# Gated linear attention and a PReLU MLP on one core: the first unit's phases and decays placed by TensorE products

## The chip, the cores and the metric

The kernel runs on one core of one Trainium2 chip. The metric is the device time of one execution in microseconds (us). A second kind of number is the span in a profile, from the first to the last instruction of one profiled execution.

## The reference, cut to what matters

```python
# q, k, v, a_re, a_im: (4 batches, 8 heads, 768 tokens, 48 channels), float32
mag = np.sqrt(a_re * a_re + a_im * a_im)
scale = np.minimum(mag, 0.999) / (mag + 1e-06)
a_re_n, a_im_n = a_re * scale, a_im * scale          # a complex gate per token and channel
for t in range(S):                                    # S_re, S_im: (B, H, 48, 48), start at zero
    new_re = ar * S_re - ai * S_im                    # ar, ai: the gate of token t, per key channel
    new_im = ar * S_im + ai * S_re
    S_re, S_im = new_re + k[t] (outer) v[t], new_im
    y[t] = q[t] @ S_re
x = y as (3072 tokens, 384)                           # heads side by side
h = x @ w_in                                          # w_in (384, 2048)
g = np.maximum(h, 0) + alpha * np.minimum(h, 0)
out = g @ w_out                                       # w_out (2048, 384); both weights arrive as 64-bit floats
```

## The kernel before, in words

The 3072 tokens are cut into 24 units of 128 tokens, six per batch. A complex gate is a magnitude and an angle. The kernel sums the angles along the tokens into a phase, turns every query and key by its phase, and so is left with real decays (magnitudes), which it multiplies up in a binary tree.

- **Gates.** `gates(g, b, c0, c1)` computes phases and decays for a group of units: group 0 is the first unit alone, group 1 the next two, group 2 the other three of batch 0, and then two groups of three for each later batch. All its operations work on the tile `room`, with the 384 rows (8 heads x 48 channels) laid out as 3 blocks of 128 partitions. VectorE (DVE) and ScalarE (ACT) take turns in it: `Abs_reciprocal_sqrt` and squares (L291 to L295), the angle (L297 to L307), its running sum (L316), cosine and sine of the phase (L319 to L351, the results being the tiles `turn` and `sine`), the magnitude (L358 to L366) and the tree of decays `dec` (L376).
- **Over DRAM.** A unit wants these numbers in another layout: heads side by side in the free dimension, channels on partitions, each channel on two neighbouring partitions (96 of them). So `gates` sends `sine` and `turn` to the DRAM tile `phs` (L342) and `dec` to `decs` (L379). The task `loads` reads them back as `PP` (L538, phases: 96 partitions, 8 heads x 129) and `T` (L545, decays: two transfers, one for the even and one for the odd partitions, 8 heads x 256).
- **Units.** `unit(u)` first multiplies the loaded queries and keys `KQ` by the phases (L625, L627 on DVE), then walks six levels of the decay tree. At each level DVE multiplies `KQ` by decays (L683), ACT copies halves of it (L706, L722), and TensorE (PE) makes small products `ps_lv` (L642), which are masked (L656 on ACT, L666 on DVE). Then come a transpose of the keys (L754, with copies L756 and L757), the state (L766, L774, L777), and the outputs `ps_y` (L792, L806), copied to `T` by ACT (L814). The first two units are moved to the layout of the MLP by PE (L823, copied at L828); the others go over DRAM (`ysc`). For the first two units three levels of the values `VL` are picked out of `V` by PE products (L587, copied at L591).
- **MLP.** Pairs of units make one block of 256 tokens. The first two blocks go through `features` (PE L874, ACT L881, DVE L883) and `outputs` (L924); the other ten through `two_features` (PE L896, ACT L905 and L909, DVE L911) and a seven-product scheme (L1014 and its folds). The weights arrive as 64-bit floats in `shared` (L440) and are turned into 32-bit ones piece by piece: ACT L460, L462, L464, then DVE L468, L470. There are 8 pieces of each weight matrix.
- **What sets the order.** Every engine executes its instructions in program order. The tasks above are generators, and each letter of the string `ORDER` advances one of them by one step: A to I are the groups of gates, J `loads`, K `half_rows`, L `loads_v`, M `pieces` (the weight loads and the loads of `start` and `alpha`), N and O the conversions of the weights, P onwards the units, n `loads_x`, o the MLP. The string was made by a planner that gave each step a cost; the kernel holds only its result. The instructions ahead of the tasks (identity, masks, small constants, almost all of it on GpSimd, POOL) stand in the order in which they are written, as the scheduler of the framework leaves them. All DMAs are issued by SyncE (SP), one queue in program order: an issue that waits holds all those behind it.
- **Two small loads that the prediction names.** `start` (L408 cleared by POOL, L415 loaded by SP) and `al` (L420, L422) stand early in SP's queue, ahead of the first weights (L440).

Of the kernel before, what the change touches and what calls it, by code (L numbers as in the profile page):

```python
# [9 lines left out]
F32 = mybir.dt.float32  # L10
# [5 lines left out]
ALU = mybir.AluOpType  # L16
# [3 lines left out]
P = 128  # L20
# [10 lines left out]
    "ABKMMAABBAAAAAAMBMJAABAMMMAAAAAAAABANABABBBBAAAAAAAAAAAAAAAAJJJMAABABNNNBBBBBBBBBBJOONOOOBPPPPJJJJBP"  # L31
    "BBBBBBBBBBPPPBNONPCJBBPPBPNJMBPPPNBBLLNLPCCCPPLLLQJPQCLCNCPPPPNPOPPPPPPPLJOCOCPPPCOPQCCNCCPJLLMLCPCL"
    "LLLQMLLCCOCJCCPOOQPQQMMCQJJPPPPPPPMLQQCCCPLOOLJQQQQQLJCCCCCQoLLLQoooNNoNNNooQQQQCRoMLoRoooQLCQRCNQQQ"
    "oQQJJCDooRoooooQRRQQQROQRoOooooNoDLLLOooRNNNCRCNCoLJQCQLooLRQQRooLCLDJNDKOCoooRoooKKQQROoQoQSDDDRRRQ"
    "QooCooooNNLDQQRRRRRoooNoRoooLRooNDMLRRLLRooooooRoLJoLRSOooooODJooooooRNDOOSoooooooJKRSOoDoRSDOOSKLoS"
    "oooSSLJRMLLDSooLNooRoooOOoNRLSLLDMJJRRRRRRRMSSSSDRRRDSSLLLLLLLJTooooDoooNooLSSSSLSJSSSSoDoooooSLSoTN"
    "OoSooooLSLLLLMNSSJDSTDSNNNNNOSOOoTOoooooooSSSSSSTTooJooTSSSSOLOJTTTooooooOTnoooDooooOOODDDDTJTooooJo"
    "oLLLDDLLLDTooooooooDTUTTJDDooooooooTTTDDJLTooooTTTTTTToooooJLUoLELLLTooTLLTDTUTTTToooJoJooooEUDDoooD"
    "DDDDTUTUTTEETEEUUUETTUooVLoUooToooooUUUUoUUooooooooUUUUUUUTooEUUoooLUoULLLoLJUooUUUEEEoUVELLJLLVLLLV"
    "VLoooKEEooooUVUUUUKVVUUUKKJVJUUJJLLLLLEVLJVVooooooooJLooVoooVVVEVoEooooooLKVKKVLLLEEoKoooooooooVVVoL"  # L40
    "LLVVVLVVooVWoVnVoJJVWWooVVVVWWWWWVVVVEWEJWWoooooVVWVWVVVVVoEoWWWoWEJoooooJJoooooooooooooWLLLLLLLEEXW"
    "WWLEXLEWEJLoXJLLLLLJooEEEWooooooooWWWWoWooooXJooooooWoXXWoooWEoXooWoEWXXoooooooEEEEooooooooEEEEXWWWW"
    "XooooooWWWXXXWWWWWoXXYLLLoXooooooooooooooooXXXXXYnXoooooooooooXXXXJJXooYooooooooXXoooXXXYXYYYXoooooY"
    "oooooooooooooooFFFFFFFLXYYXLLLLLLJLLLLooooJLJooYoooooooooFXFYXYJXXXXXXYYFZFYYZoooooooooooooooooooooJ"
    "JFLLJYYYYYYLFFoooFYYYoLLLLLLLLLZoooooooooYoYoooFYoooYYYYZFZZYYZLJLFFFFFYYZZZoooooooooooFFFFZoooLJJFo"
    "KooooooooooFYYYYYYoLYYJoJZZnZLZZLLLLFFooZoooooooooooooFFFaoZZZFFFJoFoLooFZoooaaLGZZZZooooZZLKKZFFLLL"
    "LoooooaJoooooooZoZLooooooooKZZZZLFaZaoZZooaoooooooooooooooGGJJGGGaGGaaoooooooooooooooooooooGoGaZaZZa"
    "aZoooooobFooooLoooaooooooZZZZaaGaaaobaaoooooooooooooGGooaaaaaobaoaLLJJoLLLLLLLoGbaaabbbbGaGLLLLbGGbb"
    "aaJbJooGoJboooooooooaababGboJaaaaaLLbbLJJLoooooJbJLoooooooooooooooGobbbbboonKLLLLLoGbbbbbbcoJobbccJo"
    "ooooooooobcccccccoobLbooooooooooooooooobbGcdoooooLLLLooooooooooooooGGGGGbGbGcbbcbbbbKLLLLLbGLbcKoooo"  # L50
    "ooooLccLoooLJooooooooooLLoLcGccLcoJGLGcLccoooJccdHJGooGooccooooooooooccooccoccccooooooooooGGdGGooooo"
    "oooccdddddHHdJJdcoooHdooooooooooooGoooocdcdcooodeccccddooLdoooooJHoooeoonddddddddJLdooHoHHoooooooooo"
    "ooooodLLdooHoooooodooooeoodeoooodeHeeedeooooodeoooHHHHooooooooooLLooLdooooeooooLLLLLdLLddeLdJJJddedd"
    "dddLeLLLooooLJJJLJLLLJLJeeeoooHHHHoooooooooeHHLLLeHoLoooooooeeeeooooooooeeeeeHHoooHofeoHHLHefffHoooo"
    "ooooooooooooeeeffffffeoooooooJoooooooHHHoefooHHooHHHHooooooooooeefeeefeeoefffeenoHoooooofLLLoooooooo"
    "ooooooooHHHooofffffffoooooooooofJffoJooooKffofoogLLLLggIooooogooLLoooLIfggoLgogIfIgoffIIfgLLJIJIgooo"
    "oooooooooooLLooooooooooooooffgffHgfJJfKKIffffgogIoLogooooooooooghIoooggoghhLJoooooooogoooohogggggggo"
    "ogoooLJLLLLLLLLLLghJgIhILhhgggghhIoooooooooooohIoohJJIIIIJggggggggIoooJJIInooJohooooooooooooIIIIIooo"
    "ohhhhhLiLLIJiioooLLJLLLLoooIoooooohoooooooooooooooihhhIohhhhiiLLohJooooooooiioihioooooooooooohhooooo"
    "hohohihhiLLLLjooIooooooooooojhhohIhIoooooooohhihhoiihLhhhoooooooooooooLiLioiiLIIIIIiiJiiiJoIoooooooo"  # L60
    "oooooiiioiooojoiiooiiiijjjIjjjjiojiioooLLJLLLLLLLLLoooooooooiiJIjijjioooioiiiojJJLJoooonLLLooooooooo"
    "ojooJLLooLLjkooooooooojjojjjjjjjooooooooooooooooooooooooooJJJoooooooooooooooookoLLLLLLJLjjooooookjoo"
# [35 lines left out]
def kernel(  # L98
# [44 lines left out]
    MT = MC * P  # L143
    NU = B * NCH
    GT = NCH // 2 * P
    TL = 2 * P
# [7 lines left out]
    work = ctx.enter_context(tc.tile_pool(name="work", bufs=2))  # L154
# [60 lines left out]
    g_sb = shared[:, 0:18 * MT].rearrange("p (r e) -> p r e", r=3)  # L215
    place_of = shared[:, 18 * MT - 3 * P:18 * MT]
# [13 lines left out]
    scr_of = {}  # L230
# [18 lines left out]
    def gates(g, b, c0, c1):  # L249
# [87 lines left out]
        scr = dram.tile([H * D, C, TL], F32, tag="decs", name="decs")  # L337
        phs = dram.tile([H * D, 2, n + 1], F32, tag="phs", name="phs")
# [174 lines left out]

    def loads():
        for u in range(NU):
# [18 lines left out]
            loaded[u] = L = dict(KQ=KQ)  # L534
            t = yield DMA(393, ("PP", u), takes=(R["PP"],))
# [662 lines left out]
```

## Time and profile before

| What | Value |
|---|---|
| Time, median of 3 runs | 743.08 us (741.89 to 750.89) |
| The profiled execution | 746.64 us |
| Its span | 744.9 us |
| PE busy | 675.1 us (91%) |
| DVE busy | 600.8 us (81%) |
| ACT busy | 501.3 us (67%) |
| POOL busy | 14.8 us (2%) |
| DMA queue of the loads and stores | 126.94 MB, 62.6% of 16 engines |
| Mean granted clock of PE | 0.988 |

Busy shares are averages over the whole span and hide that the kernel has stages with different limits, so the stretches of the span have to be looked at one by one. "Idle before" in a row is the idle time of the engine just ahead of it and what ended that.

### The profile page before, as it was taken

To read this page: it belongs to the slowest core of one execution; us is meant where nothing else is said; L and a number is where in the kernel's file an instruction comes from. 1 tells how busy PE (TensorE), PEld (TensorE's weight loads), DVE (VectorE), ACT (ScalarE), POOL (GpSimd) and SP (SyncE) were. 2 spreads that over 40 slices of the span, in tenths; PEclk is the share of its full clock that TensorE was granted. 3 is DMA by queue.
4 is the path that set the end of the run, shared out by engine and by line. 5 is a ranking of instruction groups with operands and counts; after the bars stand their busy time and mean duration, and the time that the engine had idled before them with its cause. 6 is when DMAs were issued, how large, how long until landed. Compare 5 with 4: busy or idle time off the path is not lost.

```text
span 744.9 us, 26879 instructions
## 1 busy us (share of the span) xinstructions
PE 675.1 (91%) x11776; PEld 582.3 (78%) x11776; DVE 600.8 (81%) x791; ACT 501.3 (67%) x899; POOL 14.8 (2%) x54
## 2 busy tenths in 40 slices
PE   0036998999999999989999999999999999999998
PEld 0025676677678888878888889989888988889997
DVE  6899999989999799989887998899876666741422
ACT  7999999976667777857676677768745354353230
POOL 6000000000000000000000000000000000000000
PEclk9997899999999999999999999999999999999999
DMA  8999987897777665786767555776738425311000
GB/s 274 235 260 266 280 279 208 213 256 235 194 195 235 178 152 152 206 226 146 199 189 227 151 120 150 241 201 169 193 83 226 111 78 149 88 40 60 0 22 22
DMA packets 157693, 128.67 MB, mean 173 GB/s; under 512 B 62696, under 2 KB 147944, under 8 KB 156136
## 3 DMA queue, kind: packets, MB, share of 16 engines
q1 hardware_dynamic: 157576, 126.94, 62.6%
q8 instruction: 93, 1.52, 0.8%
q14 instruction: 24, 0.20, 0.1%
HBM read 89.91 MB, written 34.43 MB: 167 GB/s over the span
## 4 chain that ended last, share of the span: by engine, by line
PE 57%; DVE 16%; DMA 9%; ACT 4%; issue 4%; SPq 3%; DVEq 0%; ACTq 0%
PE ps_h L896 21%; PE ps_o L1014 19%; DVE KQ L683 5%; PE ps_lv L642 4%; PE ps_y L806 3%; PE ps_kv L766 3%; DMA T<-decs 2%; DMA shared<-in_w_in_dram 2%; DMA PP<-phs 2%; PE ps_y L792 2%; PE ps_o L924 2%; PE ps_kt L754 2%; PE ps_h L874 1%; SPq L578 1%; PE ps_h L1014 1%
## 5 line engine op out<-in xcount | busy, mean ns | idle before, releaser
L896 PE MATMUL ps_h<-xT,w_in_sb 128*128 128x256 f32 x960 | 229.0, 384 | 0.8 <-DMA xT<-ysc 0.8
L896 PEld LDWEIGHTS ps_h<-xT,w_in_sb 128*128 128x128 f32 x960 | 176.6, 190 | 22.9 <-issue 1.4
L683 DVE TENSOR_TENSOR KQ<-KQ,T 96x1024 f32<-96x1024 f32 x120 | 146.0, 1216 | 19.8 <-PE ps_lv L642 10.4
L1014 PE MATMUL ps_o<-w_out_sb,shared 128*128 128x192 f32 x624 | 111.3, 329 | 1.2 <-DVE top L1020 0.8
L911 DVE TENSOR_TENSOR shared<-shared,ps_h 128x512 f32<-128x512 f32 x80 | 54.6, 682 | 70.5 <-ACT shared L909 70.5
L1014 PEld LDWEIGHTS ps_o<-w_out_sb,shared 128*128 128x128 f32 x624 | 102.2, 190 | 4.1 <-DVE top L1020 1.0
L905 ACT ACTIVATE shared<-ps_h 128x512 f32<-128x512 f32 x80 | 47.7, 596 | 68.5 <-PE ps_h L896 68.1
L1014 PE MATMUL ps_o<-shared 128*128 128x192 f32 x448 | 79.2, 329 | 0.0
L706 ACT COPY WQ<-KQ 96x1024 f32<-96x1024 f32 x48 | 49.9, 1040 | 38.0 <-DVE KQ L683 37.6
L909 ACT ACTIVATE shared<-shared,al 128x256 f32<-128x256 f32 x160 | 73.1, 502 | 2.3
L1014 PEld LDWEIGHTS ps_o<-shared 128*128 128x128 f32 x448 | 73.1, 190 | 1.6 <-DVE top L1041 0.5
L642 PE MATMUL ps_lv<-WQ 96*32 96x32 f32 x2304 | 34.3, 202 | 38.2 <-DVE WQ L625 32.1
L642 PEld LDWEIGHTS ps_lv<-WQ 96*32 96x32 f32 x2304 | 26.1, 115 | 50.5 <-DVE WQ L625 32.1
L874 PE MATMUL ps_h<-xT,w_in_sb 128*128 128x256 f32 (+1 forms) x240 | 54.0, 356 | 1.2 <-issue 1.1
L924 PE MATMUL ps_o<-w_out_sb,shared 128*128 128x384 f32 x128 | 53.1, 519 | 1.9 <-DVE shared L883 1.4
L874 PEld LDWEIGHTS ps_h<-xT,w_in_sb 128*128 128x128 f32 x240 | 41.9, 202 | 14.1 <-issue 3.2
L722 ACT COPY W<-KQ 96x512 f32<-96x512 f32 x48 | 30.8, 642 | 31.4 <-DVE KQ L683 30.2
L806 PE MATMUL ps_y<-A,VL 64*48 64x64 f32 x2304 | 45.0, 221 | 0.3 <-DMA VL<-vsc 0.3
L656 ACT ACTIVATE A<-ps_lv,columns 128x64 f32<-128x64 f32 x144 | 36.6, 332 | 12.0 <-PE ps_lv L642 11.9
L814 ACT COPY T<-ps_y 48x512 f32<-48x512 f32 x48 | 27.7, 578 | 24.0 <-PE ps_y L806 23.4
L806 PEld LDWEIGHTS ps_y<-A,VL 64*48 64x48 f32 x2304 | 36.9, 120 | 7.0 <-issue 4.9
L756 ACT COPY T<-ps_kt 128x384 f32<-128x384 f32 x48 | 23.0, 479 | 23.5 <-PE ps_kt L754 23.3
(118 smaller groups left out, 975.0 us busy)
## 6 DMA issues: line engine op xcount, KB each, us to landing
T<-decs SPq DMA_DIRECT2D x48, 384.0 KB
PP<-phs SPq DMA_DIRECT2D x24, 387.0 KB
KQ<-KQ SPq DMA_DIRECT2D x23, 384.0 KB
phs<-room SPq DMA_DIRECT2D x14, 577.5 KB
decs<-room SPq DMA_DIRECT2D x7, 1152.0 KB
VL<-vsc SPq DMA_DIRECT2D x44, 144.0 KB
shared<-in_w_in_dram SPq DMA_DIRECT2D x8, 768.0 KB
shared<-in_w_out_dram SPq DMA_DIRECT2D x8, 768.0 KB
```

The costliest lines, as they stand in the source:

```text
L642: nc.tensor.matmul(t[64 * i + j:64 * i + j + HC // 2, p], lhsT=keys(n, g), rhs=queries(n, g), start=True, stop=True)
L656: nc.scalar.activation(a[:, :, cols], t[:, :, at:at + name], AF.Copy, scale=s)
L683: nc.vector.tensor_tensor(out=x, in0=x if x0 is None else x0, in1=m, op=ALU.mult)
L706: nc.scalar.copy(z.rearrange("p i n t -> p i (n t)").rearrange("p i (m h) -> p m i h", h=h), bass.AP(tensor=KQ.tensor, offset=KQ.offset + ...
L806: nc.tensor.matmul(o, lhsT=Vp[h][64 * i:64 * i + 64, s, e_ * D:(e_ + 1) * D], rhs=a, start=False, stop=(s == 1 and h == LEVELS[-1]))
L874: nc.tensor.matmul(p, lhsT=w_in_sb[:, f // 2, kk, f % 2 * P:(f % 2 + 1) * P], rhs=x_of[m][:, kk, c * P:(c + n) * P], start=(kk == 0), stop ...
L896: nc.tensor.matmul(p[:, i], lhsT=w_in_sb[:, f // 2, kk, i * P:(i + 1) * P], rhs=x_of[m][:, kk], start=(kk == 0), stop=(kk == NK - 1))
L905: nc.scalar.activation(gt, p, AF.Relu, scale=-1.0)
L909: nc.scalar.activation(some_, some_, AF.Copy, scale=al_1[:, f + i:f + i + 1])
L911: nc.vector.tensor_tensor(out=gt, in0=gt, in1=p, op=ALU.add)
L924: nc.tensor.matmul(sums[0], lhsT=gt, rhs=w_out_sb[:, f], start=(f == start), stop=(f == stop))
L1014: nc.tensor.matmul(z, lhsT=a[:, i], rhs=w[:, i], start=i == 0, stop=i == F2 - 1)
```

## The change

For the first unit (group 0 of the gates) nothing goes over DRAM any more. The last steps of `gates(0, ...)` leave `turn`, `sine` and `dec` in `room`, and a new function `nearby` places them into `PP` and `T`: PE multiplies the blocks of `room` by slices of a shifted identity matrix (`spots`), which picks the 48 rows of a head and puts each on two partitions (decays), or the cosine on the even and the sine on the odd ones (phases). Two heads share one PSUM tile of the ring `h` (two buffers). ACT copies the four pairs of `PP` and two of the four pairs of `T`; DVE copies the other two. The matrices `spots` are made by POOL at the start, one memset and three `affine_select`. `ORDER` is a new string throughout, so all steps of all tasks may stand elsewhere; the tasks and their steps are otherwise the same.

```diff
+    spots = shared[:, 0:2 * (P + D2) * 2].rearrange("p (j c) -> p j c", j=2)
+    nc.gpsimd.memset(spots, 0.0)
+    for j, i in ((0, 0), (1, 0), (1, 1)):
+        nc.gpsimd.affine_select(out=spots[:, j], in_=spots[:, j], pattern=[[1, 2 * (P + D2)]], base=-D2 - i,
+                                channel_multiplier=-2, compare_op=ALU.not_equal, fill=1.0)
+    near = {}
     place_of = shared[:, 18 * MT - 3 * P:18 * MT]
     nc.gpsimd.memset(place_of, 0.0)
...
-        done["sine", g] = yield from send(1, ts)
+        if g:
+            done["sine", g] = yield from send(1, ts)
...
-        done["turn", g] = used = yield from send(0, t)
-        for u in range(b * NCH + c0, b * NCH + c1):
-            scr_of[u] = (scr, phs, u - b * NCH - c0)
-            done["PP", u] = used
+        if g:
+            done["turn", g] = used = yield from send(0, t)
+            for u in range(b * NCH + c0, b * NCH + c1):
+                scr_of[u] = (scr, phs, u - b * NCH - c0)
+                done["PP", u] = used
+        else:
+            near["turns"], near["decays"] = (turn, sine), dec
+            done["PP", 0] = t
...
+        if not g:
+            done["T", 0] = t
+            return
         t = yield DMA(N, t)
         nc.sync.dma_start(scr.rearrange("(t p) c s -> p t (c s)", p=P),
                           dec.rearrange("p (t c) s -> p t (c s)", t=NK))
...
+    def nearby(L):
+        L["PP"] = PP = work.tile([D2, H, P + 1], F32, tag="PP", name="PP", bufs=1)
+        L["T"] = T = work.tile([P, H, TL], F32, tag="T", name="T", bufs=2)
+        for name, key, dst, w in (("PP", "rotation", PP, P + 1), ("T", "decays", T, TL)):
+            for pair in range(HP):
+                e = yield PE(0.43 * 2.5, (name, 0), takes=(R["h"],) if pair else (R["h"], R[name]), n=6)
+                z = ps.tile([P, 2, MT], F32, tag="h", name="ps_near", bufs=2)[0:D2, :, 0:w]
+                for j in range(2):
+                    at = (2 * pair + j) * D
+                    some = [(t, at - t * P) for t in range(at // P, (at + D - 1) // P + 1)]
+                    if name == "T":
+                        some = [(near["decays"][:, t], spots[:, 1, D2 + 2 * o:2 * D2 + 2 * o]) for t, o in some]
+                    else:
+                        some = [(near["turns"][i][:, t], spots[:, 0, D2 + 2 * o - i:2 * D2 + 2 * o - i])
+                                for t, o in some for i in range(2)]
+                    for k, (rhs, lhsT) in enumerate(some):
+                        nc.tensor.matmul(z[:, j], lhsT=lhsT, rhs=rhs, start=k == 0, stop=k == len(some) - 1)
+                if name == "T" and pair % 2:
+                    t = yield DVE(2 * w, e)
+                    nc.vector.tensor_copy(dst[0:D2, 2 * pair:2 * pair + 2], z)
+                else:
+                    t = yield ACT(2 * w, e)
+                    nc.scalar.copy(dst[0:D2, 2 * pair:2 * pair + 2], z)
+                R["h"].put(t)
+            done[key, 0] = t
+        done["gates", 0] = t
...
             loaded[u] = L = dict(KQ=KQ)
+            if u == 0:
+                yield from nearby(L)
+                continue
             t = yield DMA(393, ("PP", u), takes=(R["PP"],))
```

The string `ORDER` is left out of the diff. Where the two programs stand side by side below, the lines of the kernel before are named.

More of the change, by code (lines that the diff above doesn't have):

```diff
@@ L36 @@
[L36 to L50, printed above, removed]
@@ new lines @@
+    "oCRQQQQQooooooQQRCNLLNQNoCQNQQRooKDRLLQoooCNJQNCRLQDMOOOLRCRQooooRCNNNQORCOooCQoDNNQooSRoCQQooDQQQQo"
+    "RRRQQRQLLoLLLLoDDDRooRoooLQJJLLDLKJOOoooMooRRRRRRRooooRSRooLRooROoooooRDoRDoSoRRNNNooooooooRNOORSoLo"
+    "ooooDDRLLDDLJOMROROSRSSSNSoMJRRRRRNoSDOSooooooooooooSSSoSDDDSSNooooLLLLooooooNoRRMLLLLOJSSSSSooSSNNo"
+    "ooSoSSSoDooSoSoSSDoLLLLLLLSoJJMoJTTSJOONNODOSSSSSSSooSSoOTSSLooNNoNToooooTJTonLLTLJLOTOoOOOLoLJoooJo"
+    "JToTooooooDToooooLoTTTDTDDLLDDJTDDooTooooooooLDUUooooUTTTTDLLLDTDDDoTooooooToTUUTooTTDooooTooJJELoET"
@@ new lines @@
+    "oTTDTUUTDTTTUDDDUUoooooooETTTVVVUEEETDUUUUETUULLLLLoTooooooooooooLLTTUUUUULLLLLooUUoVEUUUUooLLooEJJJ"
+    "UoooUUEUUKJKEEoooKUUUEEEEEEVEooooooooVooUVUKJKVULUUVUVoUJLLLJLVooooVooJVooooVVELEoVoVVVKoooooooooooL"
+    "oVVoVoVVVVVJoJVVWWVonooWVoLLLLoVVVEWWWLJLoEooooWVooooLLooEEEoEEoooVWJVVVWooEoVVVVVVWVVoooooWLLWWWooo"
+    "WEJoWEJLWXLLLLJooooooWWWWoooLLLLLLLWWWWWXXoWWoooooooooWXWoXXXEWWWXXXoooooooooooooWWWWLJJJXXWoWXWWWEo"
+    "EWWWooooEEEEEEEXXXnLYXoooooooooooooooooooooooooooJJLLoXXXXXXXXooooooooooooXYXXooooooXooXFLLLLooooLLL"
@@ new lines @@
+    "LYXXXXoooooooooooooFFYFYYYYXXXFYLLLYLJoFFooooooooYoKJXXYXYJYJXXXXXLFoooYYYooooooooooooLJoooYFFYJFYoo"
+    "YYLLLLLLLLoYLLooooooooKooooZLYFFYZYYYooYooYYYFFooLLooKKooooFYYZFZFJoJFooYKKKJJoooooooooYYZZYFZFoooFZ"
+    "ZZoFFFFFZKoooooooooooooooooFYZYZYYYYYooZoZZFooFooZLLLLnoooooFooooooaFZZoZFoFoZoooFoFFFaFZoooooZZoooo"
+    "oooJJLLLooooooZZZZGLLLLLLLLKooooZZJJooaFFZZZZooaZooooooooooooooooooZZaZaaZFGoGGGGGaaaoooooooooooooJJ"
+    "GooZaaaaZZZooLLaaaoooooooooooooooaaooaoaaoobbGaaaaaaZZLooLLooLLaaoJoooooooJLLLLaaabbbKGooooooooooaba"
@@ L336, in gates @@
             nc.scalar.copy(carry, turn[:, :, n])
-        scr = dram.tile([H * D, C, TL], F32, tag="decs", name="decs")
-        phs = dram.tile([H * D, 2, n + 1], F32, tag="phs", name="phs")
+        if g:
+            scr = dram.tile([H * D, C, TL], F32, tag="decs", name="decs")
+            phs = dram.tile([H * D, 2, n + 1], F32, tag="phs", name="phs")
         def send(o, after):
```

47 lines of the change are left out of this document (24 added, 23 removed).

## The prediction

> **What bounds the kernel now.** The page comes first, with the busy time and share of each engine.
>
> ```profile
> PE 675.1 (91%) x11776; PEld 582.3 (78%) x11776; DVE 600.8 (81%) x791; ACT 501.3 (67%) x899; POOL 14.8 (2%) x54
> ```
>
> PE leads, but not everywhere, so I cut the span into stretches. The columns are the stretch, its length, then busy us of PE, weight load, DVE, ACT and POOL, the clock granted to PE, the DMA share and GB/s.
>
> ```profile
> 0.00:20.00 20.00, 0.00 (x0) 0.00 (x0) 14.04 (x37) 15.74 (x26) 12.49 (x34) 1.00 0.91 271
> 20.00:32.10 12.10, 0.00 (x0) 0.00 (x0) 9.97 (x16) 11.92 (x16) 0.19 (x2) 1.00 1.01 229
> 32.10:40.00 7.90, 1.51 (x78) 1.24 (x82) 7.41 (x12) 7.84 (x10) 0.10 (x1) 1.00 0.95 229
> 40.00:65.00 25.00, 11.77 (x404) 9.67 (x398) 24.96 (x29) 24.33 (x36) 0.00 (x0) 0.99 0.97 283
> 65.00:82.00 17.00, 14.28 (x171) 11.56 (x172) 16.67 (x19) 16.85 (x28) 0.41 (x1) 0.51 1.08 271
> 82.00:110.00 28.00, 26.17 (x524) 20.16 (x526) 27.39 (x44) 26.72 (x49) 0.00 (x0) 1.00 0.96 268
> 110.00:150.00 40.00, 36.02 (x804) 27.43 (x796) 39.70 (x56) 37.58 (x62) 0.11 (x1) 1.00 0.82 218
> 150.00:700.00 550.00, 544.38 (x9601) 473.72 (x9600) 447.71 (x563) 352.02 (x663) 1.52 (x15) 1.00 0.60 164
> ```
>
> Two regimes: from 150 us PE idles 5.6 of 550 us, and whatever delays its work there delays the end. Before about 80 us PE is starved: it does nothing for 32.1 us, while ACT and DVE, from 20 us on, hardly pause. ACT idles 0.18 us between 20.0 and 32.1, and 0.67 + 0.15 + 1.28 = 2.1 us between 40 and 110. So the first MLP work comes when ACT and DVE have got through what stands ahead of it in their queues.
>
> Next, whether the trip over DRAM is what the first unit waits for. Its first DVE operation is L625, its first use of `T` L683:
>
> ```profile
> 29.98 0.96 DVE L470 CUSTOM_DVE_ANT_0 w_out_sb<-top,w_out_sb 128x1536 uint16<-128x1536 uint16 x1
> 30.85 1.21 DVE L625 TENSOR_TENSOR WQ<-KQ,PP 96x1024 f32<-96x1024 f32 x1
> 32.10 1.22 DVE L627 TENSOR_TENSOR KQ<-KQ,PP 96x1024 f32<-96x1024 f32 x1
> 33.24 0.55 DVE L691 TENSOR_TENSOR St<-St,start 96x384 f32<-96x384 f32 x1
> 33.71 1.21 DVE L683 TENSOR_TENSOR KQ<-WQ,T 96x1024 f32<-96x1024 f32 x1
> ...
> 34.93 0.85 ACT L364 ACTIVATE room<-room 128x768 f32<-128x768 f32 x1
> 35.68 0.64 ACT L722 COPY W<-KQ 96x512 f32<-96x512 f32 x1
> ```
>
> No row has an idle bracket. DVE comes to L625 straight from converting a weight, to L683 straight from L691; ACT comes to L722, the first copy of the unit, straight from the gates of group 1 (L364). `PP` and `T` were there in time: the trip is hidden behind the queues.
>
> **The change part by part.** *Order.* I set the two programs' instruction orders side by side and counted what each engine must do ahead of some landmarks. Ahead of the first L722, ACT has exactly the same operations in both, plus six copies out of `ps_near`. Ahead of the second unit's L625, and of the ninth feature's L883, DVE has the same plus two copies. So nothing of groups 1 and 2 and no weight is moved behind the first unit; at other landmarks up to the first `two_features` the sum differs by some 3 us either way. I take 0, bounds -3 and +3.
>
> *Removed.* Seven transfers: two `phs` writes, one `decs` write (as large as one read of `T`), `PP`, and two reads of `T`.
>
> ```profile
> T<-decs SPq DMA_DIRECT2D x2, 384.0 KB
> ...
> phs<-room SPq DMA_DIRECT2D x2, 193.5 KB
> PP<-phs SPq DMA_DIRECT2D x1, 387.0 KB
> ```
>
> Together 387 + 384 + 387 + 768 = 1926 KB, 1.97 MB, 7.3 us of the queue at 271 GB/s. The first unit did not wait for them, so directly they bring 0; they make room for what follows, at most 7.3 us. The next part gives that back.
>
> *Added on POOL, and with it on SP.* Here I expect most of the harm. SP issues the load of `start` only when POOL has cleared it, and `al` and all weights stand behind that issue.
>
> ```profile
> 0.94 0.42 POOL L217 MEMSET shared<- 128x384 f32 x1
> 1.44 0.29 POOL masks.py:199 TENSOR_SCALAR_AFFINE_SELECT ident<-ident 128x128 f32<-128x128 f32 x1
> 1.67 0.12 POOL L408 MEMSET start<- 96x32 f32 x1
> 1.73 0.20 POOL L173 MEMSET mask<- 128x128 f32 x1
> 1.88 0.49 POOL L220 COPY shared<-ident 48x48 f32<-48x48 f32 x2
> 2.44 0.58 POOL L228 COPY shared<-ident 128x64 f32<-128x64 f32 x3
> 2.98 1.13 POOL L174 TENSOR_SCALAR_AFFINE_SELECT mask<-mask 128x128 f32<-128x128 f32 x1
> ...
> 2.54 0.64 SPq L415 DMA_DIRECT2D start<-in_k_dram  x1
> 3.21 0.61 SPq L420 DMA_DIRECT2D al<-in_alpha_dram  x1
> 3.87 0.96 SPq L277 DMA_DIRECT2D room<-in_a_im_dram  x2
> 4.87 0.49 SPq L440 DMA_DIRECT2D shared<-in_w_in_dram  x1
> ```
>
> In the changed program the clearing of `start` stands behind a memset of 896 columns (0.42 x 896 / 384 = 0.98 us), three selects of 128x448, and the copies L220 and L228 (1.07 us). A select of 448 columns is 3.5 of the rows: between 3.5 x 0.29 = 1.0 us (POOL alone) and 3.5 x 1.13 = 4.0 us (the L174 row, beside a busy DVE). The first falls before DVE has data, the second beside its first operations, the third later: 1.0 + 2.0 + 1.4 = 4.4 us, bounds 3.1 and 11.9. So `start` is cleared at 1.67 + 0.98 + 4.4 + 1.07 = 8.1 us (6.8 to 15.6), and the first weight, two issues later (0.64 + 0.61), goes out at about 9.6 us (8.1 to 17) instead of 4.87. ACT stood waiting for that weight already:
>
> ```profile
> 11.27 0.60 ACT L328 ACTIVATE room<-room,columns 128x384 f32<-128x384 f32 x1
> 12.73 0.91 ACT L460 ACTIVATE top<-shared 128x768 f32<-128x768 f32 x1 [0.86 <-DMA shared<-in_w_in_dram]
> ```
>
> It took 7.9 us behind four loads of gates. Now those are in flight long before; 768 KB alone take 2.9 us at 271 GB/s. I take 4.9 us, so 14.5 us (11.0 to 24.9). In the new order L328 stands behind L460, not ahead, so its 0.6 us is still to be done. ACT is late by 14.5 - 12.73 + 0.6 = 2.3 us, bounds 0 and 12.7. DVE's L422 needs `al`, one issue ahead of the weight, and hides in the same hold. KQ is issued behind the weights and is needed only near 32 us. Held for 5.6 us with little in flight, the queue loses 5.6 x 271 GB/s = 1.5 MB, nearly the 1.97 MB saved: together I take 0.
>
> *Added on PE.* 20 products of 129 columns and 10 of 256. Twelve products of 256 (24 records) cost 5.19 us, 0.43 each:
>
> ```profile
> 717.05 5.19 PE ps_h L896 x24
> ```
>
> 10 x 0.43 + 20 x 0.22 = 8.7 us. The cover is PE's idle 32.1 us, and 17.3 us at half the clock fit too, since each pair waits for ACT's copies anyway: 0. Without that cover it would be 8.7.
>
> *Added on ACT and DVE.* No row has 96x258 out of PSUM; these are the nearest:
>
> ```profile
> L814 ACT COPY T<-ps_y 48x512 f32<-48x512 f32 x48 | 27.7, 578 | 24.0 <-PE ps_y L806 23.4
> L591 ACT COPY VL<-ps_vl 128x384 f32<-128x384 f32 x2 | 0.9, 464 | 0.0
> L591 ACT COPY VL<-ps_vl 128x192 f32<-128x192 f32 x2 | 0.6, 317 | 0.2 <-PE ps_vl L587 0.2
> L666 DVE TENSOR_TENSOR A<-ps_lv,mask 128x512 f32<-128x512 f32 x48 | 32.6, 680 | 0.0
> ```
>
> Between 317 and 464 ns, 258 columns make 0.37. ACT gets 4 x 0.37 + 2 x 0.58 = 2.6 us (bounds 2.4 and 3.0) ahead of L722, where it has no pause: full price. DVE's two copies (1.4 us) fall where it waits for ACT.
>
> *A new wait.* ACT's last copy of `T` is the operation right ahead of L722. DVE's L683 needs all of `T`, and L722 needs L683's result, so ACT stands for the 1.21 us of L683, where it came straight from L364. Behind it on ACT wait a weight conversion and the unit's next copies. 1.2 us, bounds 0 and 2.6 (DVE late by its own copies).
>
> *Moved on SP.* The load of group 2's `a_re` now waits for the products to be done with `room`, near 39 us by the times above; ACT wants it some 6 us later than it did: 0.
>
> Sum: L722 late by 2.3 + 2.6 + 1.2 = 6.1 us. Of ACT's 2.1 us of pauses up to 110 I let half be regained: 5 us later for the MLP, and at the end. The profiled execution took 746.64 us (span 744.9), 3.6 above the median, so 751.6 in its own terms and **748 us** against 743.08. Its own range is 743 to 754.
>
> **The rivals.** *POOL at its top price* (slower). If the selects cost what L174 cost, the first weight lands at 24.9 us: 12.7 + 2.6 + 1.2 - 1 = 15.5, 759 us. For it: selects beside a busy DVE are up to twice as dear (1.13 us in that row). Against: the first select precedes DVE's first operation. It passes 2% when the weight lands after 24 us.
>
> *PE stays longer at half its clock* (slower). Of 65 to 82 us the granted clock is 0.51, after the gap in the last of these rows (the two of ACT are for the rival that follows):
>
> ```profile
> 61.35 1.25 ACT L328 ACTIVATE room<-room,columns 128x1152 f32<-128x1152 f32 x1
> ...
> 63.52 1.07 ACT L464 ACTIVATE w_out_sb<-shared 128x768 f16<-128x768 f32 x1
> ...
> 65.66 0.58 PE L823 MATMUL ps_x<-T,shared 112*128 112x128 f32 x1 [4.49 <-ACT T L814]
> ```
>
> It ends only when PE is dense. If thinner work holds the half clock to 110 us, 26.17 us of busy time double at worst to half of it, 13 us more: 761 us; it decides when some 20 us are added. Against: the queues' content is the same.
>
> *Relief* (not slower). If POOL is cheap (hold 0) and the gap goes: ahead of the first L814 ACT has one L464 and one L328 less in the new order, 1.07 + 1.25 = 2.3 us, so the gap shrinks to about 2.2 us. Without a half clock 14.28 us of work would take 7.1, and PE, still fed by ACT, might win 7: 748 - 7 - 2.3 = 738.7. If the 1.97 MB counted in full, 731.4; with the order's 3 us, 728.
>
> The Trainium skill, "TensorE: Matmul & The Clock Gate", Part 1, says that one idle window of about 3.4 us halves the clock and that a like window of dense work restores it. The row agrees for a gap of 4.49 us; by that rule a gap of 2.2 us would keep the clock, and the time would be that of the relief.
>
> **How the numbers follow.** The forecast gets 0.38, POOL's top price 0.22 (a little over half of it past the bound, 0.13), the longer half clock 0.20, the relief 0.20 (of it 0.06 better than 2%, where all its parts meet). About 2% is what a measurement of this kernel can tell from no change, 728 to 758 us. Faster 0.06; slower 0.13 + 0.20 = 0.33; same 0.61. The range, 736 to 764, leaves out the far ends of the relief and of both slow cases.
>
> **What would show it.** Right: POOL clears `start` near 8 us and SP's next issue follows; ACT waits some 3 us for the first weight; the first L722 comes near 42 us instead of 35.68, right behind a stand of about 1.2 us; PE's products end unnoticed before it; from 150 us the windows look as before. Wrong: `start` cleared before 5 us or after 12, the first L722 before 38 us, a clock of 1.0 through 65 to 90 us or 0.5 past 95, or PE idling over 15 us after 150.

## The result, and the profile after

The change makes the kernel a little slower. On one chip, 20 runs of each: before 746.4 us (median), after 750.51 us (747.14 to 755.86), a ratio of 1.0059 with a 95% interval of 1.0035 to 1.0084. On a second chip, 12 runs of it gave 750.46 us and 1.0064 (1.0037 to 1.0091). That is some 4.5 us, well within 2%. The profiled execution of after has a span of 748.5 us, 3.6 us more than that of before. Of all runs below one, of the kernel "products alone, filled", took 2% longer than the fastest of its kernel; its median and ratio are given without that run.

In the kernel after, the lines from L217 on have moved. The names used below, before and after: L408 and L423 (clearing of `start`), L415 and L430 (its load), L440 and L455 (weight loads), L460 and L475 (first conversion of a weight), L625 and L671, L642 and L688, L683 and L729, L722 and L768 (first copy of a unit, "the first W" below), L806 and L852, L874 and L920, L924 and L970. New are L219 (selects), L546 (products), L549 and L552 (copies of DVE and ACT).

From the page of after, busy time and the two queues that matter:

```profile
PE 691.3 (92%) x11836; PEld 594.2 (79%) x11836; DVE 603.0 (81%) x793; ACT 502.2 (67%) x905; POOL 18.1 (2%) x58
...
q1 hardware_dynamic: 154792, 124.97, 60.8%
...
q8 instruction: 93, 1.52, 0.9%
```

The queue of loads and stores moved 124.97 MB instead of 126.94, the 1.97 MB that were expected. The stretches of after, cut like those of before (stretch, length, busy us of PE, weight load, DVE, ACT and POOL, granted clock, DMA share, GB/s):

```profile
32.10:40.00 7.90, 2.84 (x41) 1.44 (x39) 4.03 (x7) 4.84 (x6) 0.27 (x2) 0.86 0.78 208
40.00:65.00 25.00, 13.97 (x378) 11.11 (x381) 24.74 (x33) 24.05 (x37) 0.00 (x0) 0.50 0.78 232
65.00:82.00 17.00, 11.35 (x230) 9.49 (x231) 17.00 (x20) 16.79 (x23) 0.11 (x1) 0.70 1.02 277
...
150.00:700.00 550.00, 546.42 (x9660) 474.40 (x9659) 453.26 (x569) 357.08 (x667) 1.64 (x15) 1.00 0.61 165
```

From 150 us on PE idles 3.6 us instead of 5.6: as bound as before. The loss lies ahead. (The clock of 0.50 between 40 and 65 us must not be held against the 0.99 of before: that figure is measured only from 57.8 us on, see the last section.) Between 32.1 and 40 us DVE does 4.03 us of work where it did 7.41, ACT 4.84 where it did 7.84: both stand. The start, in the order of time per engine (POOL, SP, ACT):

```profile
2.11 1.07 POOL L219 TENSOR_SCALAR_AFFINE_SELECT shared<-shared 128x448 f32<-128x448 f32 x2
...
3.49 0.56 POOL L219 TENSOR_SCALAR_AFFINE_SELECT shared<-shared 128x448 f32<-128x448 f32 x1
...
5.58 0.12 POOL L423 MEMSET start<- 96x32 f32 x1
...
5.72 0.73 SPq L430 DMA_DIRECT2D start<-in_k_dram  x1
...
7.14 0.43 SPq L455 DMA_DIRECT2D shared<-in_w_in_dram  x1
...
12.12 0.89 ACT L475 ACTIVATE top<-shared 128x768 f32<-128x768 f32 x1 [0.85 <-DMA shared<-in_w_in_dram]
```

`start` is cleared at 5.58 us instead of 1.67, and the first weight load goes out at 7.14 instead of 4.87. ACT converts that weight at 12.12 us; before, it did so at 12.73, after waiting as long (0.86 us). The hold on POOL and SP cost ACT nothing against before. What stands between 32 and 41 us is this (PE, ACT, DVE):

```profile
16.23 4.57 PE L546 MATMUL ps_near<-room,shared 128*96 128x129 f32 x20 [16.23 <-ACT room L359]
...
27.78 5.20 PE L546 MATMUL ps_near<-room,shared 128*96 128x256 f32 x16 [1.80 <-issue]
37.02 1.38 PE L546 MATMUL ps_near<-room,shared 128*96 128x256 f32 x4 [4.04 <-ACT T L552]
...
35.66 0.84 ACT L376 ACTIVATE room<-room 128x768 f32<-128x768 f32 x1
36.41 0.56 ACT L552 COPY T<-ps_near 96x512 f32<-96x512 f32 x1
40.49 0.66 ACT L768 COPY W<-KQ 96x512 f32<-96x512 f32 x1 [3.52 <-DVE KQ L729]
...
38.44 0.69 DVE L549 COPY T<-ps_near 96x512 f32<-96x512 f32 x1 [3.77 <-PE ps_near L546]
39.23 1.22 DVE L729 TENSOR_TENSOR KQ<-WQ,T 96x1024 f32<-96x1024 f32 x1
```

The row at 37.02 is the fourth pair of `T`. It waited 4.04 us for ACT's copy of the third pair (36.41), which stands behind the gates of group 1 (L376). Behind it, one after the other: its products (1.38), DVE's copy (0.69), L729 (1.22), and only then the first W, at 40.49 us instead of 35.68, after ACT stood 3.52 us. The MLP begins 3.8 us later (first L920 at 74.41 us, first L874 at 70.59).

### The profile page after: what moved, and what is told of

It reads as the page before. It is cut to its first block, busy times and chain, and to the rows that moved or that the text cites. A ratio compares the mean times of both kernels' runs of the same rounds, so it can differ in the third digit from the quotient of the medians.

```text
span 748.5 us, 27009 instructions
## 1 busy us (share of the span) xinstructions
PE 691.3 (92%) x11836; PEld 594.2 (79%) x11836; DVE 603.0 (81%) x793; ACT 502.2 (67%) x905; POOL 18.1 (2%) x58
## 3 DMA queue, kind: packets, MB, share of 16 engines
q1 hardware_dynamic: 154792, 124.97, 60.8%
q8 instruction: 93, 1.52, 0.9%
## 4 chain that ended last, share of the span: by engine, by line
PE 73%; DVE 13%; ACT 3%; issue 2%; DMA 1%; SPq 0%; DVEq 0%; ACTq 0%
PE ps_h L942 27%; PE ps_o L1060 22%; PE ps_lv L688 6%; PE ps_y L852 5%; DVE KQ L729 4%; PE ps_h L920 3%; PE ps_y L838 3%; PE ps_kv L812 2%; PE ps_o L970 2%; PE ps_kt L800 2%; PE ps_h L1060 1%; DVE shared L1026 1%; DMA out_dram<-top 1%; DVE shared L929 1%; DVE room L337 1%
## 5 line engine op out<-in xcount | busy, mean ns | idle before, releaser
L729 DVE TENSOR_TENSOR KQ<-KQ,T 96x1024 f32<-96x1024 f32 x120 | 145.9, 1216 | 23.4 <-PE ps_lv L688 15.6
L957 DVE TENSOR_TENSOR shared<-shared,ps_h 128x512 f32<-128x512 f32 x80 | 54.6, 682 | 70.3 <-ACT shared L955 70.2
L970 PE MATMUL ps_o<-w_out_sb,shared 128*128 128x384 f32 x128 | 52.8, 518 | 2.2 <-DVE shared L929 2.0
L920 PE MATMUL ps_h<-xT,w_in_sb 128*128 128x256 f32 (+1 forms) x240 | 52.8, 356 | 0.8 <-ACT xT L874 0.4
L920 PEld LDWEIGHTS ps_h<-xT,w_in_sb 128*128 128x128 f32 x240 | 41.7, 201 | 13.6 <-issue 1.2
L768 ACT COPY W<-KQ 96x512 f32<-96x512 f32 x48 | 30.7, 640 | 32.1 <-DVE KQ L729 30.2
L852 PE MATMUL ps_y<-A,VL 64*48 64x64 f32 x2304 | 49.8, 225 | 2.1 <-issue 2.1
L852 PEld LDWEIGHTS ps_y<-A,VL 64*48 64x48 f32 x2304 | 39.3, 123 | 11.8 <-issue 8.9
L688 PEld LDWEIGHTS ps_lv<-WQ 96*32 96x32 f32 x2304 | 26.0, 114 | 23.4 <-issue 11.8
L688 PE MATMUL ps_lv<-WQ 96*32 96x32 f32 x2304 | 34.4, 201 | 8.2 <-ACT WQ L752 4.7
L546 PE MATMUL ps_near<-room,shared 128*96 128x129 f32 (+1 forms) x60 | 13.8, 399 | 24.6 <-ACT room L359 16.2
```

The source lines that it names most:

```text
L688: nc.tensor.matmul(t[64 * i + j:64 * i + j + HC // 2, p], lhsT=keys(n, g), rhs=queries(n, g), start=True, stop=True)
L729: nc.vector.tensor_tensor(out=x, in0=x if x0 is None else x0, in1=m, op=ALU.mult)
L852: nc.tensor.matmul(o, lhsT=Vp[h][64 * i:64 * i + 64, s, e_ * D:(e_ + 1) * D], rhs=a, start=False, stop=(s == 1 and h == LEVELS[-1]))
L920: nc.tensor.matmul(p, lhsT=w_in_sb[:, f // 2, kk, f % 2 * P:(f % 2 + 1) * P], rhs=x_of[m][:, kk, c * P:(c + n) * P], start=(kk == 0), stop ...
L957: nc.vector.tensor_tensor(out=gt, in0=gt, in1=p, op=ALU.add)
L970: nc.tensor.matmul(sums[0], lhsT=gt, rhs=w_out_sb[:, f], start=(f == start), stop=(f == stop))
```

## The experiments

Theory 1: the first unit is late by ACT's copies and by the wait just read, and this lateness passes to the end. Theory 2: the new order costs the time. Theory 3: POOL's work ahead of `start` does. Theory 4: the stretch at half the clock does. Theory 5 came up after the first four kernels. A summary, with the start of the first W in the profiled execution, a single one for each kernel. The two rows of after show how far that start differs between two executions of one kernel: 0.9 us. The kernels ran on several chips, each beside before on its own chip, so they are compared by their ratios and not by their medians. What each name stands for is told where the kernel comes up.

| Kernel | First W, us | Median, us | Ratio to before (95%) |
|---|---|---|---|
| before | 35.68 | 746.4, 748.86, 745.75 and 746.66 beside the others | |
| after | 40.49 | 750.51 | 1.0059 (1.0035 to 1.0084) |
| after, again | 41.38 | 750.46 | 1.0064 (1.0037 to 1.0091) |
| order alone | 40.66 | 770.46 | 1.0286 (1.0243 to 1.0329) |
| products alone | 46.54 | 790.89 | 1.0579 (1.0544 to 1.0614) |
| two banks of one tile | 40.97 | 751.47 | 1.0035 (1.0008 to 1.0062) |
| start first | 37.39 | 749.78 | 1.0001 (0.9974 to 1.0029) |
| before, shifted by 128 | 35.62 | 779.51 | 1.0452 (1.0418 to 1.0486) |
| before, shifted by 64 | 34.93 | 770.59 | 1.0335 (1.0284 to 1.0386) |
| order alone, filled | 41.63 | 753.66 | 1.0101 (1.0067 to 1.0136) |
| products alone, filled | 46.44 | 756.19 | 1.0147 (1.0115 to 1.0180) |
| own buffer | 38.21 | 747.7 | 1.0032 (1.0002 to 1.0062) |
| start first, pair on DVE | 37.29 | 745.66 | 0.9987 (0.9965 to 1.0009) |

### Order and products apart

```diff
-ORDER = (the string of the kernel before)
+ORDER = (the string of the kernel after, one "A" more behind the 26th, the 27th and the last "A", 3 "J" in place of the 16 of nearby)
```

> The kernel before, with its trip over DRAM, under the order of the kernel after (the sends set right behind the forms that they carry). Theory 1 (the products ahead of unit 0 cost the time: four ACT copies of 2.5 us and a wait of 3.5 us behind ACT's copy of T's third pair): near the kernel before, 745 to 748 us, a ratio of 0.998 to 1.003; its first L722 on ACT starts at 35 to 37 us, its first L874 at 70 to 72. Theory 2 (the order that follows unit 0 costs the time): 750 to 752 us, a ratio of 1.005 to 1.008, with the start of the first unit as early as before.

```diff
-ORDER = (the string of the kernel after)
+ORDER = (the string of the kernel before, less the three "A" of the sends, 16 "J" of nearby in place of the 3 of the trip)
```

> The kernel after, with its products and copies, under the order of the kernel before (its three steps for sends left out, all pieces of the products one after the other where the trip's pieces stood). Theory 1: at or above the kernel after, 750 to 753 us, a ratio of 1.005 to 1.009, with the first W on ACT 4 to 7 us behind the kernel before's 35.68 us. Theory 2: 745 to 748 us, a ratio of 0.998 to 1.003. Were both theories half right, this and the order alone would each show about 2 us.

Neither theory had this: the order alone took 770.46 us and the products alone 790.89, by their ratios some 21 and 43 us more than before, where the whole change costs 4.5. In the order alone the trip over DRAM is not hidden; `T` comes too late, and the first W stands at 40.66 us, as late as in after (DVE, ACT):

```profile
39.40 1.22 DVE L683 TENSOR_TENSOR KQ<-WQ,T 96x1024 f32<-96x1024 f32 x1 [4.44 <-DMA T<-decs]
...
40.66 0.66 ACT L722 COPY W<-KQ 96x512 f32<-96x512 f32 x1 [6.38 <-DVE KQ L683]
```

But after has the same lateness, and up to 112 us the two go side by side (the seventh W at 112.52 and 112.19 us). The 20 us are lost later, where the two programs have the same work in the same order. The waits of PE behind 82 us (line, what it waited for, us in total, times, longest) say where. First the longest on issue of the order alone, then of the products alone:

```profile
PE ps_lv L642 <- issue: 6.9, 5, 2.0
PE ps_y L806 <- issue: 4.5, 2, 3.5
PE ps_y L792 <- issue: 3.9, 4, 1.2
```

```profile
PE ps_lv L688 <- issue: 11.9, 6, 3.0
PE ps_y L852 <- issue: 11.3, 6, 2.8
```

"Issue" is a stand for which the profile shows no releaser. All rows of it together make 16.3 us in 12 stands for the order alone and 27.7 us in 17 for the products alone; 1.7 us in 2 for before and 4.3 us in 4 for after. One of them, in the order alone:

```profile
138.51 1.10 PE L806 MATMUL ps_y<-A,VL 64*48 64x64 f32 x61
143.13 0.94 PE L806 MATMUL ps_y<-A,VL 64*48 64x64 f32 x35 [3.52 <-issue]
144.01 2.93 PE L874 MATMUL ps_h<-xT,w_in_sb 128*128 128x256 f32 x6
```

61 and 35 short products, a stand of 3.52 us among them, and then six L874 at 2.93 us where six take 1.46 at full clock: the stand also halves the clock.

Theory 5 is made from the second queue of the page: 93 packets and 1.52 MB on the instruction queue, 16,384 bytes each. The program before has about 23,800 instructions on PE (11776 weight loads, as many products and some 240 waits): 256 for every packet, 64 bytes each. So the theory is that PE's code arrives in blocks of 256 instructions while it runs. In nine traces of this case (before, after twice, and the six kernels on order and blocks) there are 41 stands on issue longer than 1.2 us behind 82 us, and every one of them ends 1.2 to 1.7 us after a packet of that queue has landed. Their place is the same too: counted along PE's loads, products and waits, in order of time and modulo 256, all 41 come at the 194th or 195th instruction. And the blocks cut at that place differ: behind 82 us the shortest takes PE 3.7 to 4.0 us in before, in after and in the two filled kernels below, but 1.8 to 2.0 us in the four kernels with many stands. Where short products fill a block, PE is through it before the next one is there.

### Where the blocks of code end

These kernels put tiny products ahead of everything on PE, in a PSUM tile that nobody reads. They change no work and no order, only the place at which the blocks end:

```diff
+    filler = ps.tile([P, 2, 512], F32, tag="y", name="ps_filler")
+    for _ in range(32):
+        nc.tensor.matmul(filler[0:32, 0, 0:1], lhsT=ident[0:32, 0:32], rhs=ident[0:32, 0:1], start=True, stop=True)
     with tc.manual_schedule():
```

> The kernel before with 32 products of 32x1 from a constant put ahead of everything on PE, into a PSUM tile that nobody reads: 128 more instructions in front of PE's stream (two loads and two products each), next to no work, and long done before the first unit. Theory 5 (PE's code arrives in blocks of 256 instructions, 16 KB each on the instruction queue, one block ahead; where 256 instructions run in under some 4 us PE stands for the next block, and a stand halves its clock; the order is tuned to where the blocks end, which 128 more instructions move by half a block): 770 to 795 us, a ratio of 1.03 to 1.06, with 15 to 30 us of stands of PE on issue behind 82 us where the kernel before has 1.7. Theories 1 to 4, in which code plays no part: the kernel before's time, a ratio of 0.998 to 1.003.

779.51 us, a ratio of 1.0452. The first unit is where it was (35.62 us). The waits of PE behind 82 us, and one stand:

```profile
PE ps_lv L642 <- issue: 10.5, 7, 3.3
PE ps_y L806 <- issue: 8.7, 6, 2.6
PE ps_y L792 <- issue: 5.1, 3, 3.6
```

```profile
325.74 1.16 PE L766 MATMUL ps_kv<-V,T 64*64 64x48 f32 x64
326.83 0.46 PE L642 MATMUL ps_lv<-WQ 96*32 96x32 f32 x32
327.11 0.49 PE L642 MATMUL ps_lv<-KQ,W 96*32 96x32 f32 x32
327.53 0.42 PE L792 MATMUL ps_y<-KQ,St 96*48 96x64 f32 x6
331.52 1.65 PE L792 MATMUL ps_y<-KQ,St 96*48 96x64 f32 x26 [3.57 <-issue]
333.10 4.20 PE L1014 MATMUL ps_o<-w_out_sb,shared 128*128 128x192 f32 x13
```

As expected: 27.3 us in 19 stands instead of 1.7 in 2. In the stretch shown 134 short products, 268 instructions, run in 2.2 us, PE stands for 3.57, and of the long products that follow 13 take 4.20 us (16 took 2.87 in before). Between 82 us and the last microseconds the clock records show half for 27 us in all, in before nowhere.

The two mixed kernels again, now with fillers that put the ends of their blocks where the kernels after and before have them ("filled" in the table; `range(30)` and `range(34)` in the same three lines):

> The kernel before with its trip over DRAM, under the order of the kernel after, with 30 such products of 32x1 ahead of everything on PE, which stand for the 120 instructions of the products that it lacks, so that its blocks of code end where the kernel after's do. Theory 5: the order alone lost its 21 us only to the blocks; 748 to 752 us, within 3 us of the kernel after on the same chip, 2 to 6 us of stands on issue. Its first L722 still comes near 40.7 us, since with this order the trip is not hidden (DVE waits 4.4 us for T). Theory 2 (the order with the trip is slow by itself): 766 to 773 us, as without the 30 products.

> The products under the order of the kernel before, with 34 products of 32x1 ahead of everything on PE: with the products' own 120 these make 256 instructions, so that its blocks of code end where the kernel before's do. Theory 5: the stands on issue fall from 27 us to under 6, and of the 43 us of loss there stays what the late first unit costs; the first W is 10.9 us late, and if all of that comes through (theory 1) 756 to 760 us, if half of it is made up, 750 to 755. Without theory 5: 788 to 794 us, as without the 34 products.

> The kernel after, unchanged, beside the three others on one chip, as their common yardstick: 750 to 752 us, a ratio of 1.004 to 1.008; PE's stands in the trace with no releaser but its own issue add up to 3 to 5 us behind 82 us, as in its first trace (4.0 us in three).

Adding work brought the ratio of the one from 1.0286 down to 1.0101 and that of the other from 1.0579 to 1.0147, some 14 and 32 us. The second median, 756.19, is at the edge of what was expected, with 3.8 us of stands; the first is above it, 753.66 instead of 748 to 752 and 3.2 us above after on the same chip, with 9.0 us of stands instead of 2 to 6. After itself showed 6.2 us in five, a little more than expected, in a profiled execution that was its longest (span 754.5 us). Of the products alone, filled, one row is left on issue:

```profile
PE ps_h L920 <- issue: 3.8, 1, 3.8
```

So theory 2 falls: the 21 us of the order alone were for the most part the place of the blocks, and that after's order can be as fast as before's is shown by the last kernel below (0.9987). With after's order the trip (753.66) is not faster than the products (750.46; the intervals overlap), and their traces go side by side to the last L911 and L957, at 734.27 and 733.51 us. With before's order the products cost 11 us (1.0147), about the 10.8 us by which their first W is late. Of the combinations tried, each way of the first unit did best with its own order, and each order with the place of the blocks that its own kernel has.

A quarter of a block (`range(16)` ahead of the kernel before):

> The kernel before with 16 products of 32x1 ahead of everything on PE, 64 instructions, a quarter of a block of code. Theory 5: laid over the trace of the kernel before, ends of blocks moved by 64 instructions give 18 us of blocks that run in under 3.9 us, against 8 us where they are and 30 us when moved by 128; so about half of what the shift by 128 cost (33 us): 757 to 766 us, a ratio of 1.015 to 1.027, and 10 to 18 us of stands on issue. If it were the fillers themselves that cost: a quarter to a half as much as well, but then the kernels whose fillers restored the place of the blocks would not have become faster.

770.59 us, 1.0335: a miss in size. 22.1 us of stands in 15, not 10 to 18, and three quarters of the loss at half the shift. The count of blocks that run too fast, laid over the trace of before, finds that a shift hurts but not how much.

### The first unit

```diff
-                z = ps.tile([P, 2, MT], F32, tag="h", name="ps_near", bufs=2)[0:D2, :, 0:w]
+                if name == "T" and pair >= 2:
+                    if pair == 2:
+                        zy = ps.tile([P, 2, 512], F32, tag="y", name="ps_near_y")
+                    z = zy[0:D2, pair - 2].rearrange("p (j w) -> p j w", j=2)
+                else:
+                    z = ps.tile([P, 2, MT], F32, tag="h", name="ps_near", bufs=2)[0:D2, :, 0:w]
```

> The kernel after, but T's third and fourth pair of products go to the two banks of another PSUM tile, so that the fourth no longer waits for ACT's copy of the third. Theory 1: the first W on ACT starts at 38 to 39 us instead of 40.49, its idle time of 3.52 us ahead of it falls to 1 to 1.5, and the end comes about 2 us earlier than the kernel after: 747.5 to 749.5 us, a ratio of 1.002 to 1.004. Theory 2, and theory 3 (POOL's clearing and selects hold the loads and ACT's first conversion): the kernel after's time, 750 to 751 us. Theory 4 (what counts is how long PE runs at half its clock, so that any earlier start of unit 0 is lost to a longer half-clock stretch): the first W earlier, the end unchanged within 1 us.

This experiment did not do what it was for. The wait stayed: the fourth pair still began only behind ACT's copy of the third, out of the other bank of what is now one tile. The first W came at 40.97 us. The ratio, 1.0035, has an interval that overlaps that of after and says nothing.

```profile
36.86 2.02 PE L551 MATMUL ps_near_y<-room,shared 128*96 128x256 f32 x4 [5.30 <-ACT T L557]
```

With a tile for the fourth pair alone it does:

```diff
-                z = ps.tile([P, 2, MT], F32, tag="h", name="ps_near", bufs=2)[0:D2, :, 0:w]
+                if name == "T" and pair == 3:
+                    z = ps.tile([P, 2, 512], F32, tag="y", name="ps_near_y")[0:D2, 0].rearrange("p (j w) -> p j w", j=2)
+                else:
+                    z = ps.tile([P, 2, MT], F32, tag="h", name="ps_near", bufs=2)[0:D2, :, 0:w]
```

> The kernel after, but T's fourth pair of products gets a PSUM tile of its own, instead of the buffer that the third pair has just been given (in the earlier try both pairs lay in one tile, and the wait stayed). POOL's order is as in the kernel after. Theory 1: the fourth pair is done near 32 us, DVE's second copy stands near 34.7 instead of 38.44, ACT's idle time ahead of the first W falls from 3.52 to 1.3 us, the first W comes at 38.2 to 38.5, and the end 2 us earlier than the kernel after: a ratio of 1.002 to 1.005. Theory 3 (POOL's clearing and selects are what counts, and made all the gain of the kernel with start cleared first): the kernel after's ratio, 1.005 to 1.008.

```profile
32.42 1.03 PE L549 MATMUL ps_near_y<-room,shared 128*96 128x256 f32 x4
...
34.53 0.68 DVE L552 COPY T<-ps_near_y 96x512 f32<-96x512 f32 x1
36.96 1.22 DVE L732 TENSOR_TENSOR KQ<-WQ,T 96x1024 f32<-96x1024 f32 x1 [1.75 <-ACT T L555]
...
38.21 0.66 ACT L771 COPY W<-KQ 96x512 f32<-96x512 f32 x1 [1.29 <-DVE KQ L732]
```

The fourth pair begins at 32.42 us, DVE's copy stands at 34.53 instead of 38.44, the wait ahead of the first W falls from 3.52 to 1.29, the first W comes 2.3 us earlier, and the ratio is 1.0032, in the middle of what was expected. The interval overlaps that of after; the place of the wait is shown by the trace, the 2 us at the end only made likely.

```diff
+    start = consts.tile([D2, B, H], F32, tag="start")
+    nc.gpsimd.memset(start, 0.0)
     ident = consts.tile([P, P], F32, tag="ident")
...
-    start = consts.tile([D2, B, H], F32, tag="start")
-    nc.gpsimd.memset(start, 0.0)
```

> The kernel after, with start's clearing ahead of everything else on POOL, so that neither SP's store from it nor the loads queued behind that store wait for it. Theory 1: the first weight lands 1 to 2 us earlier, ACT's first conversion too at most, and the end moves by less than 1 us: 749.5 to 751 us, a ratio of 1.004 to 1.007. Theory 3: 746 to 748 us, most of the difference gone.

1.0001: the whole loss is gone, as theory 3 had it, but not for its reason alone. The trace shows two differences: ACT converts the first weight 0.9 us earlier and without a wait, and in this program the fourth pair was given the other buffer, so that it waits for DVE's copy at 32.51 us and not for ACT's. By the first W the hold is the smaller part: the own buffer alone brought it 2.3 us forward, this kernel another 0.8. The end does not tell the two apart (1.0059, 1.0032 and 1.0001, with intervals that overlap from step to step), so what the hold costs there stays open. ACT's first conversion and first W:

```profile
11.22 0.89 ACT L475 ACTIVATE top<-shared 128x768 f32<-128x768 f32 x1
...
37.39 0.66 ACT L768 COPY W<-KQ 96x512 f32<-96x512 f32 x1 [1.29 <-DVE KQ L729]
```

Last the version to which these point, start first and the third pair of `T` on DVE:

```diff
-                if name == "T" and pair % 2:
+                if name == "T" and pair:
```

> The kernel after with start cleared first on POOL, and with T's third pair copied by DVE instead of ACT (DVE stood idle there; ACT has one copy of 0.56 us less ahead of the first W). Theory 1: the first W at 36.2 to 36.8 us, 1 us earlier than with start cleared first alone and within 1 us of the kernel before's 35.68; at the end 1 us less too, a ratio of 0.997 to 1.001. If what DVE takes on is paid there: as with start cleared first alone, 0.998 to 1.003.

```profile
34.73 1.28 DVE L549 COPY T<-ps_near 96x512 f32<-96x512 f32 x2
...
37.29 0.66 ACT L768 COPY W<-KQ 96x512 f32<-96x512 f32 x1 [0.67 <-DVE KQ L729]
```

0.9987 (0.9965 to 1.0009): faster than after, not to be told from before. The copies stand in a row on DVE, and ACT waits 0.67 us. The first W is at 37.29 us and not at the expected 36.2 to 36.8, since in this execution the first steps of the gates ran 1 us later (ACT's first conversion at 12.26 instead of 11.22 us).

Theory 4 falls with the two kernels that clear `start` first: their first W came earlier, and their end did not stay where it was (intervals apart from those of after). Taken together, the lateness of the first W passes to the end about one for one where it is large: 10.8 us gave 11.0 (8.6 to 13.4), 4.8 and 5.7 gave 4.4 and 4.8, 2.5 gave 2.4. The two banks of one tile do not fit as well: 5.3 us gave 2.6 (0.6 to 4.6). The two smallest, 1.7 and 1.6, gave 0.1 and -1.0, each with some 2 us to either side: there may be some 2 us of gain in the change that the lateness eats up. That is not shown, and the rule of one for one is a fit to starts that are uncertain by 1 us, beside stands on issue that differ by some 3 us between these kernels.

## Why the prediction came out

748 us was forecast against 743.08, +5 us; the chips gave +4.1 to +4.7. The path was right: the first W late behind ACT's copies and a wait for DVE, and that lateness passed on to the end. That the sum came out is luck, since of its three terms two were too large and one too small. ACT ahead of the first W, in before and after (columns as above):

```profile
0.00:35.68 35.68, 0.66 (x32) 0.52 (x32) 27.31 (x55) 31.19 (x44) 12.68 (x36) 1.00 0.93 249
0.00:40.48 40.48, 14.41 (x92) 11.03 (x92) 29.13 (x58) 32.67 (x50) 16.23 (x41) 0.92 0.78 215
```

Of the 4.8 us, 1.5 are more work of ACT and 3.3 more idle time. By the steps of the prediction:

- *Hold on POOL and SP*, 2.3 us (bounds 0 and 12.7): nothing against before; the weight converted 0.6 us earlier makes up for L334, 0.6 us, which stands behind L475 as said. The selects were priced by rows of 128x128, 1.0 to 2.0 us each; two together took 1.07, the third 0.56. `start` was cleared at 5.58 us, below the lower bound of 6.8. The dear row, L174 at 2.98 us, was read as one beside a busy DVE; but DVE's first operation on data begins at 3.54 us there, and the third select of after, beside the same operation (3.53 us), was not dear.
- *ACT's copies*, 2.6 us: four of 0.35 and two of 0.56, 2.5 us by their rows, as forecast. But rows of one engine overlap (before's L364 ends at 35.78 us, the first W begins at 35.68), and ACT's busy time ahead of the first W grew by 1.5 us only.
- *The new wait*, 1.2 us (bounds 0 and 2.6): 3.52 us, above the bound. This is the term that was too small. The step took it that all pairs were there when ACT came to its last copy, and that only L683 stood in between. The two-buffer ring gave the fourth pair the buffer of the third, so its products and DVE's copy came behind ACT's copy as well. The two extra terms, 1.38 and 0.69 us, are rows of after; that the buffer causes them is shown by the kernel with its own buffer, where the stand falls to 1.29 us.
- *PE's products*, 0: they took 13.8 us of busy time instead of 8.7 and cost PE nothing, but the fourth pair's 1.38 us is on the path through that wait.
- *Removed*, 0: the bytes were right (1.97 MB), the count was not; 387 + 384 + 387 + 768 KB are six transfers, not seven.
- *Order*, 0 (-3 to +3): right, and incomplete as a way to look. ACT's work ahead of the first W is the same but for the six copies, as said (44 and 50 operations above). But an order also says where PE's blocks of code end, which the prediction did not see: the order alone costs 14 us more when 120 instructions are missing ahead of it (1.0286 against 1.0101).
- *First W late by 2.3 + 2.6 + 1.2 = 6.1 us*: 0 + 1.5 + 3.3 = 4.8. *Half of ACT's pauses regained, MLP late by 5*: 3.8.
- *The rivals.* POOL's top price: not seen. A longer half clock: not seen; it ended at 78.7 us, in before at 81.7. The relief: its first half came true, the wait of 4.49 us ahead of `ps_x` is gone. Its second half didn't, as the next rows show (PE of after):

```profile
64.92 0.34 PE L688 MATMUL ps_lv<-WQ 96*32 96x32 f32 x10
66.92 0.36 PE L688 MATMUL ps_lv<-WQ 96*32 96x32 f32 x19 [1.66 <-issue]
...
67.73 2.32 PE L869 MATMUL ps_x<-T,shared 112*128 112x128 f32 x12
```

A stand on issue of 1.66 us, at the 195th instruction of a block like the others, has taken the place of the wait, and from 68.4 to 78.7 us the clock is at half again. The prediction cited the Trainium skill, "TensorE: Matmul & The Clock Gate", Part 1, for the rule that an idle window of about 3.4 us halves the clock. From it the prediction took that a gap of 2.2 us would keep it. Here a gap of 1.66 us was enough: in the 3.41 us up to the change PE was busy for 1.63. The measurement decides. Not every such gap does it: of the shifted kernel's stands one of 1.59 us kept the clock and one of 1.10 lost it.

## What to carry to other kernels

When a tile is handed on through a ring of two buffers, look up which buffer each step gets and who has to leave it first; here that, and not the added copies' own time, was the largest single part of the lateness (2.3 of 4.8 us). Where PE runs hundreds of short products, its code is itself a load that can be late: before you blame an order for a loss, look at the stands on issue, and shift PE's stream by some tiny products to see whether the place of the blocks is what you measure. A part of a change that was tuned as a whole cannot be judged by undoing it alone, unless PE's instruction count is kept.

## What the runs showed of the hardware that was not expected

- PE stands for its own code. 256 instructions are one 16 KB packet; 128 more instructions at the start, with next to no work in them, cost 33.8 us (745.75 to 779.51), and 256 - 120 = 136 more took some 32 us off another kernel (1.0579 to 1.0147).
- Between 132 and 145 us every kernel but before has a stand on issue of 1.3 to 4.4 us, also where the block ahead of it was not short: in after PE took 5.3 us for that block and still stood for 1.88, since the packet started only 4.2 us after PE had entered the block. Why it is late there stays open.
- The granted clock is not to be read before its first record. For before that is at 57.77 us. The stretch from 32.1 to 40 us is given as 1.00, yet 32 products of the same form took 0.66 us in it, and still at 46.73 us, and 0.46 later. In after they took 0.66 us at a recorded half (41.20 us). So before, too, ran at half its clock there, though not up to 65 us as after did:

```profile
32.12 0.66 PE L642 MATMUL ps_lv<-WQ 96*32 96x32 f32 x32 [32.12 <-DVE WQ L625]
...
58.21 0.46 PE L642 MATMUL ps_lv<-WQ 96*32 96x32 f32 x32
```

- A select of 128x448 on POOL took 0.56 to 0.76 us in these traces, no more than many of 128x128 (0.29 to 1.51 us): its price did not go by its columns.
